# One SBUF ring tile taken earlier, the gate's rounds spaced wider, three transposes of c moved, and one pool shifted, in a fused attention and two-MoE kernel

## The chip, the cores and the metric

The kernel runs on one core of a Trainium2 chip, which has eight. The metric is device microseconds (us) for one execution, start to end; lower is better. Only one core is used, so there is no traffic between cores.

## What is computed

Three stages in a row, all in float32, whose intermediate results never leave the core:

```python
def reference(q, k, v, ...):
    out_up = repeat(sm_attn(mean4(q), mean4(k), mean4(v)), 4)       # pooled attention, 4 tokens to one
    out_local = softmax(where(|i - j| < 4, q k^T / 8, -1e9)) @ v     # attention in a narrow band
    x = (out_up + out_local) as [2304 tokens, 512]
    # soft MoE: 8 experts, 4 slots each
    logits = x @ phi                                # 2304 x 32
    d = softmax(logits, over tokens); slot_input = d.T @ x
    slot_out[e] = relu(slot_input[e] @ w1[e]) @ w2[e]
    x = softmax(logits, over slots) @ slot_out      # c @ slot_out, c is 2304 x 32
    # second MoE: 8 experts, every token through every expert
    P = exp(x @ w_gate - max)
    for _ in range(8):                              # Sinkhorn rounds
        P /= P.sum(1, keepdims=True) + 1e-9
        P /= P.sum(0, keepdims=True) + 1e-9
        P *= N / E
    out = sum over e of P[:, e:e + 1] * (relu(x @ w1[e]) @ w2[e])
```

The second MoE carries nearly all the arithmetic: for each of 8 experts, 2304 x 512 x 1024 and 2304 x 1024 x 512. Its input x has rank 32 (it is c times 32 slot outputs), and the kernel uses that: the first product is (c scaled by the gate) times a small matrix of 32 rows.

## The kernel before

**Stages.** Attention over 16 pairs of heads comes first, then the soft MoE, then the second MoE, which is one long loop over `seq`, 72 steps of (e, p): expert e outside, p one of nine blocks of 256 tokens inside. The instructions of all engines are written out by hand in one order; each engine runs its own in that order and waits for semaphores.

**The first expert (e = 0, steps n = 0 to 8).** Step p runs `y_first(p)`: 48 matmuls of 512 columns that multiply hidden values (tiles `s75` and `s63`, each a high and a low part) with the weights `whi` and `wlo`, in two halves c = 0 and c = 1 of the hidden units. `hidden(0, p, c)` makes the hidden values. The last half, (p, c) = (8, 1), puts them in a tile of their own, `hl` (L957), because `s75` and `s63` are wanted by the second expert by then.

**The gate.** Beside these matmuls runs a generator, `side`: `gate()`, then eight times `sink()`, one Sinkhorn round. It is called once for every two matmuls of `y_first`; each `yield` is one such place. A round puts four short DVE instructions on the gate's tile `pg` (L1132 to L1135), passes 6 places, puts a matmul `sp` with a tile of ones on PE (L1139), passes 2, puts five DVE instructions (L1145 to L1149), passes 5.

**The other experts (e = 1 to 7).** Step (e, p) runs `y_pair(e, p)`: seven products of a Strassen-like scheme, each 12 matmuls of 256 columns, 84 in all, in four PSUM banks: products 7 and 5, then 6 and 3, then 1, then 4 and 2. The stationary operand comes from `s75`, `s63` or `d` (made by `hidden`, `sums`, `direct_hi`, `direct_lo`), the moving one from the weight tile W[e, n] of that product. Hooks at given matmul counts k call the work for the next steps: `hidden` at 2 and 14, `sums` from 19 on, `direct_hi` at 79, and so on.

**The ring of weight tiles.** `w_tile` hands out tiles of 8 KB a partition in turn from a ring of ten: seven buffers of pool `wp`, then three of pool `tp`. Tile number i reuses the buffer of tile i - 10, and its first write waits until the last reader of that one is done. The order decides which tile meets which. Tiles 0 to 7 are the first expert's weights. Each later expert takes seven, in the order 7, 5, 6 (`w_early`, an ACT copy and a POOL subtraction each, in steps p = 5, 6 and 7 of the expert before), 3, 1, 4 (`w_late`, in step p = 8 of the expert before) and 2 (step p = 0 of its own). `hl` is taken when it is written, in step (0, 8): it is tile 11, between 7, 5, 6 (8, 9, 10) and 3, 1, 4, 2 (12 to 15) of expert 1. Expert 2's are 16 to 22.

**c times the gate.** `scale_c(e, p)` multiplies c with the gate's column on POOL into `crp` (two buffers); `turn_c(e, p)` transposes it on PE into the PSUM tile `cq` (pool `xq`, a single buffer), copies it with ACT (L936) and subtracts with DVE (L937) into `ce`, which `hidden(e, p, ...)` reads. For expert 1 these are called in step (0, 8), at k = 2 to 24; `hidden(1, 0, 0)` follows at k = 12.

**Places in SBUF.** The pools lie one behind the other: `wp`, `acc`, `tp`, `rp`, `mm`, `op`. Up to `mm` the sizes are multiples of 512 bytes a partition. `mm` holds `ones` (512), `stack_r` (512), `low_rows` (4, which takes 32), `skew` (32, a tile that no instruction uses), `rs` (72, takes 96), `cs`, `gm`, `g1`, `gn` (32 each), `wf` (4096) and two `crp` (1024 each). So `op`, with the stationary operands, begins 288 bytes past a multiple of 512 from where the weight tiles begin.

Of the kernel before, what the change touches and what calls it, by code (L numbers as in the profile page):

```python
# [8 lines left out]
FP32 = mybir.dt.float32  # L9
# [41 lines left out]
def attn_moe_moe_kernel(  # L51
# [13 lines left out]
    nc = tc.nc  # L65
    B, H, S, D = q.shape
    N, DM = out.shape
    E, _, F = w1a.shape
    NS = phi.shape[1]
    SPE = NS // E  # L70
    HP = H // 2
    NT = N // 128
# [718 lines left out]
    mm = ctx.enter_context(tc.tile_pool(name="mm", bufs=1, reuse_waits="tile"))  # L791
    op = ctx.enter_context(tc.tile_pool(name="op", bufs=3, reuse_waits="tile"))
# [8 lines left out]
    def w_tile(name, dtype=FP32R):  # L801
        nonlocal nt_
        pool = wp if nt_ % NTW < NW else tp
        nt_ += 1
        return pool.tile([128, 2048], dtype, name=name, tag="w")
# [105 lines left out]

    O = {}
    H = {}
    ce = {}
    crp = {}

# [25 lines left out]
    def o_tile(tag, n):  # L942
        return op.tile([128, 2, 2, 128 * n], FP32R, name=tag, tag=tag, bufs=n)

    def hidden(e, p, c):

        ps = hq.tile([128, 2, 512], FP32, name="h", tag="h")
        if e == 0:
            for f in range(4):
                g = 4 * c + f  # L950
                nc.tensor.matmul(  # L951
                    out=ps[:, f // 2, 256 * (f % 2):256 * (f % 2) + 256], lhsT=a4s[:, 0, 128 * g:128 * g + 128],
                    rhs=c4[:, 256 * p:256 * p + 256], start=True, stop=True,
                )
            if (p, c) == (NP - 1, 1):

                t = w_tile("hl")  # L957
                hi, lo = t[:, 0:1024], t[:, 1024:2048]
            else:
                hi, lo = (o_tile(n, 2).rearrange("p a b x -> p (a b x)") for n in ("s75", "s63"))  # L960
            O[0, p, c] = hi, lo
            for j in range(2):
                h = slice(512 * j, 512 * j + 512)
                nc.scalar.activation(out=hi[:, h], in_=ps[:, j], func=ACTF.Relu)  # L964
                relu(lo[:, h], ps[:, j], hi[:, h].bitcast(FP32), ALU.subtract)
            return
        for j in range(2):
            for k in range(2):
                g = 2 * c + j + 4 * k
                nc.tensor.matmul(  # L970
                    out=ps[:, j, 256 * k:256 * k + 256], lhsT=a4s[:, e % 2, 128 * g:128 * g + 128],
                    rhs=ce[e, p], start=True, stop=True,
                )
        r21 = op.tile([128, 2, 128], FP32, name="r21", tag="r21", bufs=2)
        x = op.tile([128, 2, 2, 256], FP32, name="xs", tag="xs", bufs=2)
        H[e, p, c] = ps, x
        A21, A11, A22, A12 = (ps[:, :, 128 * i:128 * i + 128] for i in range(4))
        s3, s1, s2, s4 = (x[:, i // 2, :, 128 * (i % 2):128 * (i % 2) + 128] for i in range(4))
        nc.scalar.activation(out=r21, in_=A21, func=ACTF.Relu)  # L979
        now = c == 0 or (e, p) == (1, 0)  # L980
        if now:
            direct_hi(e, p, c)
        relu(s3, A11, r21, ALU.subtract)
        relu(s1, A22, r21, ALU.add)
        relu(s2, A11, s1, ALU.subtract)
        relu(s4, A12, s2, ALU.add)
        if now:
            direct_lo(e, p, c)

    def sums(e, p, c, i):  # L990

        t = o_tile(("s75", "s63")[i], 2)
        v = H[e, p, c][1][:, i]
        for j, n in enumerate(("75", "63")[i]):
# [4 lines left out]
    def direct_hi(e, p, c):  # L999
        t = H[e, p, c, "d"] = o_tile("d", 3)  # L1000
        for j, n in enumerate("142"):
# [87 lines left out]
            out=out[128 * t:128 * t + 128, :], in_=acc[:, p, h:h + 2, :].rearrange("p q d -> p (q d)")  # L1089
        )  # L1090

    ones = mm.tile([128, 128], FP32, name="ones")
    nc.vector.memset(ones, 1.0)
    stack_r = mm.tile([128, 4, 32], FP32R, name="stack_r")
    nc.vector.tensor_copy(out=stack_r, in_=stack)
    low_rows = mm.tile([128, 1], FP32, name="low_rows")
    mm.tile([128, 8], FP32, name="skew")
    for i in range(4):
        nc.vector.memset(low_rows[32 * i:32 * i + 32], -1.0 if i % 2 else 0.0)

# [30 lines left out]
    def sink():  # L1131
        nc.vector.tensor_reduce(out=rs[:, :, 0], in_=pg, axis=AX.X, op=ALU.add)  # L1132
        nc.vector.tensor_scalar(out=rs, in0=rs, scalar1=EPS, scalar2=None, op0=ALU.add)
        nc.vector.reciprocal(out=rs, in_=rs)
        nc.vector.tensor_tensor(out=pg, in0=pg, in1=rs.to_broadcast([128, NT, E]), op=ALU.mult)  # L1135
        for _ in range(6):
            yield
        sp = xq.tile([128, NT, E], FP32, name="sp", tag="x")
        nc.tensor.matmul(  # L1139
            out=sp.rearrange("p t e -> p (t e)"), lhsT=ones, rhs=pg.rearrange("p t e -> p (t e)"),  # L1140
            start=True, stop=True,
        )
        for _ in range(2):
            yield
        nc.vector.tensor_reduce(out=cs_[:, 0, :], in_=sp.rearrange("p t e -> p e t"), axis=AX.X, op=ALU.add)  # L1145
        nc.vector.tensor_scalar(out=cs_, in0=cs_, scalar1=EPS, scalar2=None, op0=ALU.add)
        nc.vector.reciprocal(out=cs_, in_=cs_)
        nc.vector.tensor_tensor(out=pg, in0=pg, in1=cs_.to_broadcast([128, NT, E]), op=ALU.mult)
        nc.vector.tensor_scalar(out=pg, in0=pg, scalar1=float(N) / E, scalar2=None, op0=ALU.mult)  # L1149
        for _ in range(5):  # L1150
            yield
# [43 lines left out]
    for n, (e, p) in enumerate(seq):  # L1195
        nx, nx3, nx4 = at(n + 1), at(n + 3), at(n + 4)
        hooks = {}

        def hook(k, f, *a):
            hooks.setdefault(k, []).append((f, a))  # L1200

        total = 48 if e == 0 else 84
        fr = (lambda x: x * total // 84)
        if e == 0:
            if n:
                hook(2, hidden, 0, p, 1)
            if n < NP - 1:
                hook(26, hidden, *nx, 0)
            else:
                for k, f, *a in (  # L1210
                    (12, hidden, 0), (14, sums, 0, 0), (22, hidden, 1), (26, sums, 1, 0), (28, sums, 0, 1),
                    (30, sums, 1, 1),
                ):
                    hook(k, f, *nx, *a)
        elif nx:
            for k, f, *a in (
                (2, hidden, 0), (14, hidden, 1), (19, sums, 0, 0), (26, sums, 1, 0), (43, sums, 0, 1),
                (50, sums, 1, 1), (79, direct_hi, 1), (79, direct_lo, 1),
            ):
                hook(k, f, *nx, *a)  # L1220

        if n == NP - 2:

            def first_c():
                make_cx()
                for i in range(2):
                    scale_c(1, i)

            hook(total - 8, first_c)
        if n == NP - 1:  # L1230
            for i in range(2):
                hook(2 + 6 * i, turn_c, 1, i)
                hook(8 + 6 * i, scale_c, 1, 2 + i)
            hook(18, turn_c, 1, 2)
            hook(24, scale_c, 1, 4)
        elif n >= NP:
            if nx3:
                hook(64, turn_c, *nx3)
            if nx4:
                hook(70, scale_c, *nx4)  # L1240
        if nx and nx[0] == 1:
            hook(fr(40), scale_first, nx[1])
        if e + 1 < E:
            if p == 0:
                hook(60, load_w1, e + 1) if e else hook(12, load_w1, e + 1)
            if p in (2, 3):
                hook(fr(10), a_part, e + 1, p - 2)
                hook(fr(34), a_sum, e + 1, p - 2)
            if p == 3:
                hook(fr(30), load_w2, e + 1, 0)  # L1250
                hook(fr(30), load_w2, e + 1, 1)
            if p == 4:
                early = w_early(e + 1)
                hook(fr(60), next, early)
            if p in (5, 6, 7):
                hook(fr(28), next, early)
                hook(fr(56), next, early)
            if p == 8:
                for x, m in (28, "3"), (52, "1"), (72, "4"):
                    hook(fr(x), w_late, e + 1, m)  # L1260
        if e and p == 0:
            hook(8, w_late, e, "2")
        k = 0
        for _ in (y_first(p) if e == 0 else y_pair(e, p)):
            k += 1
            if e == 0 and k % 2 == 0 and (n or k > 6):
                next(side, None)
            if n == 0 and k <= 12:
                if k % 3 == 0:
                    next(soon, None)  # L1270
                if k == 6:
                    hidden(0, 0, 1)
            for f, a in hooks.pop(k, ()):
                f(*a)
        assert not hooks, (e, p, list(hooks))
# [28 lines left out]
```

## Time and profile before

| | us |
|---|---|
| median of three runs | 1084.28 |
| lowest and highest | 1084.22, 1086.52 |
| the profiled execution | 1083.03 |
| its span, first to last instruction | 1081.2 |
| PE busy in the span | 1025.5 (95%) |
| DVE, POOL, ACT busy | 779.0, 649.4, 540.0 |

The profile is one execution. PE is TensorE's matmuls, PEld its weight loads, DVE VectorE, ACT ScalarE, POOL GpSimd. L1064 stands for line 1064 of the kernel. The attention takes the span up to about 190 us, the soft MoE up to about 219, the first expert of the second MoE about 223 to 350, the other seven experts 350 to 1076. The granted clock of TensorE is 1.00 (2.4 GHz) in nearly all of the second MoE.

### The profile page before, as it was taken

What the parts mean: (1) busy time and instruction counts of PE and PEld (TensorE: products, weight loads), DVE (VectorE), ACT (ScalarE), POOL (GpSimd) and SP (SyncE); (2) the same over time, 40 slices, a digit from 0 to 9 for tenths busy, and PEclk for the clock granted to TensorE, in tenths of its full rate; (3) what the DMA queues carried; (4) which work ended last, traced back from release to release, by engine and by line L of the source; (5) the groups of instructions that cost most, each with busy time, mean ns of one, the idle gap of its engine ahead of it and who ended that gap; (6) DMA issues with size and microseconds to landing.
All of it is one profiled execution on the core that took longest, in us unless ns stands there. A gap on an engine that the chain in (4) does not pass through costs nothing.

```text
span 1081.2 us, 22771 instructions
## 1 busy us (share of the span) xinstructions
PE 1025.5 (95%) x9033; PEld 928.0 (86%) x9033; DVE 779.0 (72%) x1521; ACT 540.0 (50%) x1040; POOL 649.4 (60%) x543
## 2 busy tenths in 40 slices
PE   6887988889999999899999999999999999999998
PEld 5675753367787899899999999999999999999998
DVE  4997872155654677677778778778777787788996
ACT  4986750132225556554564456455545564455442
POOL 5655341020044859974897589659946994699452
PEclk8999997889999999999999999999999999999999
DMA  9999998941100220022003100310210022000111
GB/s 190 174 183 234 260 332 320 386 169 40 39 1 1 79 78 2 2 79 79 1 1 118 40 2 8 111 41 1 79 57 24 2 78 79 2 2 21 59 40 60
DMA packets 95919, 93.84 MB, mean 87 GB/s; under 512 B 59076, under 2 KB 64836, under 8 KB 95812
## 3 DMA queue, kind: packets, MB, share of 16 engines
q1 hardware_dynamic: 95812, 92.37, 30.3%
q8 instruction: 72, 1.18, 0.5%
q14 instruction: 35, 0.29, 0.1%
HBM read 87.64 MB, written 4.72 MB: 85 GB/s over the span
## 4 chain that ended last, share of the span: by engine, by line
PE 76%; DVE 3%; POOL 2%; DMA 1%; issue 1%; ACT 1%; ACTq 0%; DVEq 0%; POOLq 0%
PE m L1064 56%; PE y L1021 7%; PE h L970 5%; PE h L712 2%; PE ap L885 1%; DMA w1s<-in_moe_w_dram 1%; PE cq L933 1%; POOL wt L842 1%; POOL s L842 1%; PE h L951 1%; PE so L761 1%; PE as L901 1%; DVE xs L940 1%; DVE acc L1051 0%; DVE d L940 0%
## 5 line engine op out<-in xcount | busy, mean ns | idle before, releaser
L842 POOL TENSOR_TENSOR s<-xs,s 128x512 fp32r<-128x512 f32 x252 | 323.0, 1299 | 192.7 <-ACT s L996 192.7
L1064 PE MATMUL m<-wt,s 128*128 128x256 f32 x3024 | 394.9, 282 | 1.3 <-POOL s L842 1.3
L1064 PEld LDWEIGHTS m<-wt,s 128*128 128x128 f32 x3024 | 374.2, 189 | 12.9 <-issue 10.1
L1064 PE MATMUL m<-wt,d 128*128 128x256 f32 x2268 | 292.3, 283 | 1.2 <-DVE acc L1051 1.2
L1064 PEld LDWEIGHTS m<-wt,d 128*128 128x128 f32 x2268 | 276.6, 188 | 1.6 <-PE m L1064 1.5
L1051 DVE TENSOR_TENSOR acc<-acc,m 128x512 f32<-128x512 f32 x315 | 215.2, 683 | 23.3 <-PE m L1064 10.9
L996 ACT ACTIVATE s<-xs 128x512 fp32r<-128x512 f32 x252 | 155.9, 630 | 104.5 <-DVE xs L940 69.3
L940 DVE SCALAR_TENSOR_TENSOR d<-h,d 128x768 fp32r<-128x768 f32 x126 | 120.0, 953 | 92.8 <-ACT d L1003 92.8
L1003 ACT ACTIVATE d<-h 128x768 fp32r<-128x768 f32 x126 | 102.2, 811 | 74.7 <-PE m L1064 74.7
L940 DVE SCALAR_TENSOR_TENSOR xs<-h,xs 128x256 f32<-128x256 f32 x252 | 107.0, 425 | 8.6
L940 DVE SCALAR_TENSOR_TENSOR xs<-h,r 128x256 f32<-128x256 f32 x252 | 94.7, 418 | 20.8 <-issue 13.3
L1021 PE MATMUL y<-whi,s 128*128 128x512 f32 x272 | 89.4, 407 | 2.1 <-ACT whi L835 2.1
L979 ACT ACTIVATE r<-h 128x256 f32<-128x256 f32 x126 | 48.3, 384 | 83.7 <-PE h L970 83.5
L842 POOL TENSOR_TENSOR wt<-w2r,wt 128x1024 fp32r<-128x1024 f32 x35 | 84.1, 2413 | 7.6 <-ACT wt L848 7.6
L970 PE MATMUL h<-cx,a4s 128*128 128x256 f32 x504 | 81.0, 283 | 2.9 <-DVE d L940 2.9
L970 PEld LDWEIGHTS h<-cx,a4s 128*128 128x128 f32 x504 | 69.4, 190 | 3.3 <-DVE d L940 3.1
L1021 PEld LDWEIGHTS y<-whi,s 128*128 128x128 f32 x272 | 51.0, 192 | 12.5 <-ACT whi L835 2.5
L842 POOL TENSOR_TENSOR wf<-w2r 128x1024 f32<-128x1024 f32 x14 | 33.8, 2414 | 42.9 <-issue 42.9
L964 ACT ACTIVATE s<-h 128x512 fp32r<-128x512 f32 x34 | 20.3, 598 | 73.4 <-PE h L951 56.8
L1021 PE MATMUL y<-wlo,s 128*128 128x512 f32 x136 | 55.4, 408 | 0.0
L936 ACT ACTIVATE cx<-cq 128x256 fp32r<-128x256 f32 x63 | 24.1, 382 | 60.8 <-PE cq L933 60.8
L842 POOL TENSOR_TENSOR wt<-wf,wt 128x1024 fp32r<-128x1024 f32 x14 | 33.7, 2410 | 32.6 <-ACT wt L848 32.6
(206 smaller groups left out, 1152.6 us busy)
## 6 DMA issues: line engine op xcount, KB each, us to landing
wa<-in_moe_w_dram SPq DMA_DIRECT2D x32, 1024.0 KB, 9.4
w1r<-in_moe_w_dram SPq DMA_DIRECT2D x14, 1024.0 KB
w2r<-in_moe_w_dram SPq DMA_DIRECT2D x14, 1024.0 KB, 5.0
vw<-in_v_dram SPq DMA_DIRECT2D x62, 96.0 KB, 6.1
kn<-in_k_dram SPq DMA_DIRECT2D x32, 144.0 KB, 6.0
vg<-in_v_dram SPq DMA_DIRECT2D x16, 288.0 KB
out_dram<-acc SPq DMA_DIRECT2D x18, 256.0 KB, 2.0
qn<-in_q_dram SPq DMA_DIRECT2D x20, 144.0 KB, 7.0
```

The lines of the kernel that those rows point to most:

```text
L712: nc.tensor.matmul(out=h1[32 * j:32 * j + 32, a, :], lhsT=slt[:, j, e, :], rhs=w[:, j % 2, 512 * a:512 * a + 512], start=(e == 0), stop=(e ...
L842: eng.tensor_tensor(out=out, in0=x, in1=y, op=ALU.subtract)
L936: nc.scalar.activation(out=r, in_=cp, func=ACTF.Copy)
L940: nc.vector.scalar_tensor_tensor(out=out, in0=ps_, scalar=0.0, in1=in1, op0=ALU.max, op1=op1)
L964: nc.scalar.activation(out=hi[:, h], in_=ps[:, j], func=ACTF.Relu)
L970: nc.tensor.matmul(out=ps[:, j, 256 * k:256 * k + 256], lhsT=a4s[:, e % 2, 128 * g:128 * g + 128], rhs=ce[e, p], start=True, stop=True,)
L979: nc.scalar.activation(out=r21, in_=A21, func=ACTF.Relu)
L996: nc.scalar.activation(out=t[:, 0], in_=v, func=ACTF.Copy)
L1003: nc.scalar.activation(out=t[:, 0], in_=H[e, p, c][0][:, :, 128:512], func=ACTF.Relu)
L1021: nc.tensor.matmul(out=ys[i], lhsT=l, rhs=r, start=(c == 0 and n == 0), stop=(c == 1 and n == 11))
L1051: nc.vector.tensor_tensor(out=v, in0=v, in1=ps, op=op_)
L1064: nc.tensor.matmul(out=ps[:, place], lhsT=l, rhs=W[e, n][:, r, j, :], start=(m == 0), stop=(m == 11))
```

## The change

Four edits. First, `hl`'s tile is taken from the ring at the start of step n = 3, ahead of expert 1's tiles; it becomes tile 8, and expert 1's 7, 5, 6 become 9, 10, 11. All numbers from 12 on are as before. No instruction moves for that. Second, `ones` moves from `mm` to the first buffer of `r21` in `op`, and `skew` grows from 32 to 480 bytes, so `op` begins 64 bytes lower. Third, a Sinkhorn round passes 9 places instead of 6 ahead of its matmul. Fourth, in step (0, 8) the calls of `turn_c` for blocks 0, 1, 2 go from k = 2, 8, 18 to 6, 11, 20 and those of `scale_c` for blocks 2, 3, 4 from 8, 14, 24 to 8, 13, 22.

```diff
+    hl = []
@@ hidden
             if (p, c) == (NP - 1, 1):
-                t = w_tile("hl")
+                t = hl[0]
                 hi, lo = t[:, 0:1024], t[:, 1024:2048]
@@
-    ones = mm.tile([128, 128], FP32, name="ones")
+    ones = op.tile([128, 128], FP32, name="ones", tag="r21", bufs=2)
     nc.vector.memset(ones, 1.0)
@@
-    mm.tile([128, 8], FP32, name="skew")
+    mm.tile([128, 120], FP32, name="skew")
@@ sink
-        for _ in range(6):
+        for _ in range(9):
             yield
         sp = xq.tile([128, NT, E], FP32, name="sp", tag="x")
@@ the loop over seq
         if n == NP - 1:
-            for i in range(2):
-                hook(2 + 6 * i, turn_c, 1, i)
-                hook(8 + 6 * i, scale_c, 1, 2 + i)
-            hook(18, turn_c, 1, 2)
-            hook(24, scale_c, 1, 4)
+            for k, i in (6, 0), (11, 1), (20, 2):
+                hook(k, turn_c, 1, i)
+                hook(k + 2, scale_c, 1, 2 + i)
@@
+        if n == 3:
+            hl.append(w_tile("hl"))
```

## Rows read from the trace of the kernel before

**Rows 1.** Page: engines' busy us; costly group: busy, mean ns, idle before.

```profile
PE 1025.5 (95%) x9033; PEld 928.0 (86%) x9033; DVE 779.0 (72%) x1521; ACT 540.0 (50%) x1040; POOL 649.4 (60%) x543
...
L1064 PE MATMUL m<-wt,s 128*128 128x256 f32 x3024 | 394.9, 282 | 1.3 <-POOL s L842 1.3
```

**Rows 2.** Waits of PE, 226 to 1077 us: total, times, longest.

```profile
PE h L970 <- DVE d L940: 2.9, 1, 2.9
PE y L1021 <- ACT whi L835: 2.1, 1, 2.1
PE cq L933 <- DVE cx L937: 1.4, 1, 1.4
PE m L1064 <- POOL s L842: 1.3, 1, 1.3
PE m L1064 <- DVE acc L1051: 1.2, 2, 0.6
PE sp L1139 <- DVE pg L1135: 1.1, 2, 0.8
```

**Rows 3.** Chain of work, 440 to 470 us: start, us, what.

```profile
442.25 0.22 PE cq L933 x2
...
449.90 1.22 PE h L970 x4
...
457.90 0.22 PE cq L933 x2
...
469.01 0.22 PE cq L933 x2
```

**Rows 4.** Timeline (start, us, instruction, [idle before]); windows (five engines' busy, clock, DMA).

```profile
446.83 1.06 ACT L848 ACTIVATE wt<-wf 128x1024 fp32r<-128x1024 f32 x1 [4.90 <-PE m L1064]
...
442.00:458.00 16.00, 13.06 (x100) 12.86 (x99) 9.06 (x17) 7.81 (x12) 14.31 (x12) 0.89 0.00 1
```

**Rows 5.** Timeline at the two late Sinkhorn matmuls.

```profile
256.43 0.48 PE L1139 MATMUL sp<-pg,ones 128*128 128x144 f32 x2 [0.27 <-DVE pg L1135]
...
278.36 2.41 POOL L842 TENSOR_TENSOR wf<-w2r 128x1024 f32<-128x1024 f32 x1 [42.94 <-issue]
278.94 1.86 DVE L1133 TENSOR_SCALAR rs<-rs 128x18 f32<-128x18 f32 x1
...
281.59 0.48 PE L1139 MATMUL sp<-pg,ones 128*128 128x144 f32 x2 [0.83 <-DVE pg L1135]
```

**Rows 6.** Timeline of step (0, 8): the second transpose of c.

```profile
338.66 0.43 DVE L937 TENSOR_TENSOR cx<-cq,cx 64x256 fp32r<-64x256 f32 x1
...
339.23 0.41 PE L933 MATMUL cq<-ident,crp 128*128 128x128 f32 x2 [1.43 <-DVE cx L937]
...
340.40 0.64 PE L970 MATMUL h<-cx,a4s 128*128 128x256 f32 x4
```

**Rows 7.** Timeline of POOL in step (0, 8).

```profile
343.75 1.30 POOL L842 TENSOR_TENSOR s<-xs,s 128x512 fp32r<-128x512 f32 x1 [6.58 <-ACT s L996]
345.01 0.62 POOL L922 TENSOR_TENSOR crp<-lnat,pg 128x256 f32<-128x256 f32 x1
```

**Rows 8.** Matmul rates: chain 1050 to 1082, then `y` and `as`.

```profile
1058.21 18.24 PE m L1064 x154
...
325.72 0.40 PE L1021 MATMUL y<-wlo,s 128*128 128x512 f32 x1
...
328.52 0.40 PE L1021 MATMUL y<-wlo,s 128*128 128x512 f32 x1
...
346.20 0.39 PE L1021 MATMUL y<-wlo,hl 128*128 128x512 f32 x1
...
348.92 0.39 PE L1021 MATMUL y<-wlo,hl 128*128 128x512 f32 x1
...
262.55 0.47 PE as L901 x2
...
488.87 0.47 PE as L901 x2
```

## The prediction

> **What bounds the kernel now.** I read the page first. PE is busy 95% of the span [rows 1], and from about 350 us on its largest group, the `m` matmuls of L1064, runs almost without idle time: 1.3 us of waiting over 3024 matmuls. So two things can move the time: the few places where PE stands still, and the rate at which its matmuls follow each other. Next I read PE's waits over the second MoE [rows 2]. The reader sees a short list: 10.0 us in six kinds, with 2.9 us in one single wait of an `h` matmul for DVE at the top. Three of the six kinds are touched by the change: that one, `cq <- DVE cx` with 1.4, and `sp <- DVE pg` with 1.1. `m <- POOL s` and `m <- DVE acc` lie behind POOL in the turn from the first expert to the second, and are touched in passing. The wait for `whi` lies at the start of the first expert and is not touched.
>
> **The ring tile (edit 1).** In the chain, `cq` of one step comes at 442.25, of the next at 457.90, of the one after at 469.01 [rows 3]: one step takes 15.65 us, its neighbour 11.11, so 15.65 - 11.11 = 4.54 us are lost in it. The cause stands in ACT's row [rows 4]: the split of a weight tile (L848) begins at 446.83, after 4.90 us of waiting for an `m` matmul of PE. By the code this is `w_early`'s third split for expert 2, product 6, called at k = 56 of step (1, 7). It is tile 18, and tile 18 - 10 = 8 is product 7 of expert 1, last read at k = 12 of step (1, 8). ACT works in order, so its `cx` copy and `direct_hi` for the next half queue up behind the split, DVE's `direct_lo` behind those, and PE's second `hidden` at k = 14 behind DVE: that is the 2.9 us [rows 2]. While PE stands, its clock falls: the window 442 to 458 has a mean granted clock of 0.89 [rows 4], so part of it ran at 1.2 GHz, and the first `h` group after the wait takes 1.22 us. The other 4.54 - 2.9 = 1.6 us are that.
>
> With `hl` as tile 8, tile 18 meets `hl`, whose last reader is the last matmul of step (0, 8), some 90 us earlier. The split then starts when ACT comes to it. What is late next? The later tiles meet product 7 (tile 19, split at k = 28, freed at k = 12), 5 (split at 52, freed at 24), 6 (72, 36) and 3 (8 of the next step, 48), the pattern that all later experts have, and they show no such wait (the `h` wait occurs once) [rows 2]. `hl` itself takes over a buffer of `tp` without an earlier `w_tile` in it; expert 1's 5 and 6 move onto the two `w1s`, last read before the first `y`. I take the whole: **-4.5 us**. If a new wait took its place, it would be at most the same again.
>
> **The gate's places (edit 3).** PE waited 1.1 us in two of the eight rounds, 0.27 and 0.83 [rows 5]. Three places more are six `y` matmuls, at 2.80 us for 12 [rows 8] 1.40 us, more than either wait. The four DVE instructions and the DVE work queued among them get that much longer; PE runs `y` meanwhile. The gate ends eight times 1.40 = 11 us later, at about 314 us; its first reader on POOL (`crp` for expert 1, called at k = 40 of step (0, 7)) comes some 20 us behind. The second wait was made by one slow instruction: a TENSOR_SCALAR of 18 numbers took 1.86 us beside a POOL subtraction of 2.41 us [rows 5]. The rounds that move later run into more of these splits, so I let one such wait of up to 0.8 us come back in the bound. **-1.1 us**, between -1.4 (the clean gaps) and -0.3.
>
> The Trainium skill ("SBUF — State Buffer", section "Who interferes with whom") says that DVE and GpSimd share a pair of ports, exclusively for a whole instruction, so the second to start waits for the first. The long row is in accord with that; by it a round that meets a POOL split pays up to the split's length, and three places would not cover every meeting. That changes this term by less than 1 us.
>
> **The turns of c (edit 4).** `cq` has one buffer. The second transpose waited 1.43 us for DVE's subtraction of the first, which sat behind `hl`'s two evictions and began at 338.66 [rows 6]. This chain starts from `hidden(0, 8, 1)` and does not move: it ends at 338.66 + 0.43 = 339.09. What changes is how much PE does before it must wait: with 6 and 11 instead of 2 and 8, three more matmuls of 0.233 us (0.70 us) come ahead of the wait, and `hidden(1, 0, 0)` at k = 12 stands one matmul behind the second transpose instead of four. It was issued at 340.40 [rows 6]; now about 339.7. So PE still waits, but 0.7 us less. POOL gains more. It was idle 6.58 us before the first `s` subtraction at 343.75 and then ran `crp` for 0.62 us at 345.01 [rows 7]; that `crp` (block 3, from k = 14, behind `sums`, to 13, ahead of it) now falls into the idle time. POOL's following work, on which PE waits with `m <- POOL s` (1.3 us) and, through DVE, `m <- DVE acc` [rows 2], comes 0.7 + 0.6 = 1.3 us earlier. PE cannot gain more than that there: **-1.2 us**, between -0.6 (only the first wait) and -2.0 (all of the two waits that follow, less what PE itself comes earlier). If POOL's idle time were not there, the `crp` would cost its 0.6 us again.
>
> **The shift of 64 bytes (edit 2).** From the sizes in the code, `op` began 288 bytes past the weight tiles, modulo 512; with `ones` out (512) and `skew` 448 larger it is 224, or the weights 288 past `op`. No instruction is added. The only question is whether PE's rate depends on where its two operands lie. `m` runs at 18.24 / 154 = 118.4 ns; `y` from `s75` and `s63` (288 apart) at 2.80 / 12 = 233 ns, `y` from `hl` (same pool as its weights, 0 apart) at 2.72 / 12 = 227 ns [rows 8]. So it may, by 6 ns in 233, or 2.8%. The nearest row to the new distance is `as`: for the first experts its operands are `stack_r` and `aps`, 224 apart, and two matmuls take 0.47 us; from the third expert on they are 0 apart and also take 0.47 [rows 8]. So distance 224 costs nothing there against 0, within 5 ns. I take **0**. The ends: the seven experts have 63 x 84 = 5292 `m` matmuls, 627 us at 118.4 ns, and 2.8% of them is 17.5 us either way.
>
> The Trainium skill ("TensorE: Matmul & The Clock Gate", section "Step-by-step: what each phase is for") says that weight loads and the moving operand have separate SBUF read ports and so do not slow each other; by that rule the shift is worth nothing, as I take it. The two rates of `y` speak against it being the whole story, so I keep the ends.
>
> **The sum.** -4.5 - 1.1 - 1.2 + 0 = -6.8 us. The profiled execution took 1083.03, 1.8 around its span, and becomes 1076.2; it lay 1.25 below the median, so on the median 1084.28 the forecast is 1077.5 us.
>
> **Rivals.** (a) The shift speeds PE up: `op`'s new distance is as good for `m` as 0 is for `y`. For it: the 227 ns. Against: `as`. By 1 ns in 118 it is worth 5.3 us, in full 17.5: 1060 to 1075, most likely about 1070. (b) The shift slows PE down: weight loads and moving stream collide more. Place: every `m` matmul. It decides against the kernel from 6.8 us / 5292 = 1.3 ns a matmul on; at half the bound, 1.6 ns, +8.7 us, 1086.2; in full 1095. For it: PE's rate is the bound for 700 us, so nothing hides it. Against: the `as` row. (c) The ring only passes the wait on: another split in steps (1, 7) and (1, 8) meets a busy tile. Then the -4.5 are lost and 1082.0 remains. Against: the freed and split counts above. (d) `skew`, which no instruction uses, takes no room; then the distance stays and the forecast stands, since its term is 0.
>
> **How the numbers follow.** Forecast with (d): 0.54; (a) 0.25; (b) 0.13; (c) 0.08. The range takes the gain of (a) down to 1066 (beyond lies about 0.07) and (b) up to 1083 (beyond lies 0.1): 1066 to 1083. What a measurement can tell from no change is about 0.2%, 2.2 us: faster is below 1082.1, slower above 1086.4. Faster: the forecast, (a), half of (c) and a little of (b): 0.85. Same: half of (c) and the part of (b) between 1082 and 1086: 0.09. Slower: the rest of (b): 0.06.
>
> **What the new profile would show.** Edit 1: no ACT wait at L848 near 440 us, steps of 11.1 us throughout from (1, 4) on, clock 1.00. Edit 3: no `sp <- DVE pg`. Edit 4: `cq <- DVE cx` near 1 us instead of 1.4, `crp` ahead of the first `s` on POOL, `m <- POOL s` under 0.8. Edit 2: 154 `m` matmuls at the end in 18.24 us; 17.5 would mean rival (a), 18.6 rival (b). The forecast is wrong if that last number moves.

## The result, and the profile after

The kernel after takes 1070.26 us (median of four runs, 1066.78 to 1071.43) against 1085.40 for the kernel before: a ratio of 0.985, with a 95% interval of 0.982 to 0.988. It is 15.1 us faster where 6.8 were forecast: the time lies inside the range of the prediction, but the gain is 2.2 times the one forecast. The profiled execution took 1071.43 us, with a span of 1069.7.

First the page of the kernel after (busy us of the engines; then the costliest matmul group, as in [rows 1]). A line is 1 to 2 higher in number than before from `hidden` on.

```profile
PE 1018.8 (95%) x9033; PEld 920.0 (86%) x9033; DVE 780.5 (73%) x1521; ACT 539.1 (50%) x1040; POOL 649.4 (61%) x543
...
L1065 PE MATMUL m<-wt,s 128*128 128x256 f32 x3024 | 389.1, 280 | 1.0 <-POOL s L842 1.0
```

PE is busy 6.7 us less with the same 9033 instructions, and the 3024 `m` matmuls of this group 5.8 us less. That speaks for more than waits that went away: the matmuls themselves follow each other faster. The waits of PE in the second MoE, in total, times and the longest, answer to [rows 2] (the one for `whi`, at the start of the first expert, left out):

```profile
PE m L1065 <- DVE acc L1052: 1.1, 2, 0.7
PE cq L934 <- DVE cx L938: 1.0, 1, 1.0
PE m L1065 <- POOL s L842: 1.0, 1, 1.0
PE m L1065 <- POOL wt L842: 0.5, 1, 0.5
```

The 2.9 us of `h` and the 1.1 us of `sp` are gone; `cq` fell from 1.4 to 1.0, and `m <- POOL s` from 1.3 to 1.0 (the prediction wanted it under 0.8); one wait is new, of `m` for `wt` on POOL. The chain of work, in one ordinary step and at the end, answers to [rows 3] and [rows 8]:

```profile
545.50 0.22 PE cq L934 x2
...
550.64 5.84 PE m L1065 x50
556.48 0.22 PE cq L934 x2
...
1046.94 17.98 PE m L1065 x154
```

A step is 556.48 - 545.50 = 10.98 us, before 11.11; the last 154 `m` matmuls run at 116.8 ns, before 118.4.

To see where the 15 us come from I take the start of the first matmul of each step from the records of both profiled executions; a step's length is the difference of two.

| stretch | before | after | change |
|---|---|---|---|
| up to the first `y` (attention, soft MoE) | 226.02 | 229.30 | +3.28 |
| (0, 0) | 16.51 | 16.09 | -0.42 |
| (0, 1) to (0, 7), the gate's | 92.29 | 90.82 | -1.47 |
| (0, 8) and (1, 0), the turns of c | 27.91 | 26.61 | -1.30 |
| (1, 8) and (2, 0), the ring | 26.77 | 23.50 | -3.27 |
| an ordinary step, for example (5, 5) | 11.11 | 10.98 | -0.13 |
| (2, 1) to the last `m` | 604.72 | 597.08 | -7.64 |

The first two rows are no part of the change: over the executions profiled for this study the first `y` starts between 220.2 and 229.6 us, and step (0, 0) takes 16.0 to 17.0. The steps (1, 1) to (1, 7), which the table leaves out, take 0.72 us less. From the first `y` to the last `m` it is 850.14 against 835.33, 14.8 us less, and 8 of them (63 steps of 0.13) are the pace of `m`. In the last row 0.92 us belong to the single step (7, 1), 11.90 us before and 10.98 after, of which more below.

### The profile page after: what moved, and what is told of

Read it like the earlier page. It is cut to its first block, busy times and chain, and to the rows that moved or that the text cites. A ratio compares the mean times of both kernels' runs of the same rounds, so it can differ in the third digit from the quotient of the medians.

```text
span 1069.7 us, 22765 instructions
## 1 busy us (share of the span) xinstructions
PE 1018.8 (95%) x9033; PEld 920.0 (86%) x9033; DVE 780.5 (73%) x1521; ACT 539.1 (50%) x1040; POOL 649.4 (61%) x543
## 4 chain that ended last, share of the span: by engine, by line
PE 79%; POOL 7%; DMA 5%; DVE 3%; ACT 2%; SPq 2%; issue 1%; POOLq 0%; ACTq 0%; DVEq 0%
PE m L1065 52%; PE y L1022 9%; PE h L971 5%; POOL s L842 3%; POOL wt L842 2%; DMA kn<-in_k_dram 2%; PE ap L885 1%; PE h L712 1%; DMA w1s<-in_moe_w_dram 1%; PE cq L934 1%; DMA wa<-in_moe_w_dram 1%; PE loc L465 1%; PE h L952 1%; PE so L761 1%; SPq L222 1%
## 5 line engine op out<-in xcount | busy, mean ns | idle before, releaser
L1065 PE MATMUL m<-wt,s 128*128 128x256 f32 x3024 | 389.1, 280 | 1.0 <-POOL s L842 1.0
L1065 PEld LDWEIGHTS m<-wt,s 128*128 128x128 f32 x3024 | 369.5, 188 | 12.5 <-issue 10.1
L1065 PE MATMUL m<-wt,d 128*128 128x256 f32 x2268 | 289.4, 282 | 1.6 <-DVE acc L1052 1.1
L1065 PEld LDWEIGHTS m<-wt,d 128*128 128x128 f32 x2268 | 273.8, 188 | 2.2 <-PE m L1065 1.5
```

The lines of the kernel that those rows point to most:

```text
L1065: nc.tensor.matmul(out=ps[:, place], lhsT=l, rhs=W[e, n][:, r, j, :], start=(m == 0), stop=(m == 11))
```

## The experiments

### The ring alone

```diff
 # before, plus
+        if n == 3:
+            hl.append(w_tile("hl"))
```

> The kernel before with edit 1 alone (hl takes its ring tile at n = 3). Theory: the 4.54 us of step (1, 8) go, but POOL, which had used that stall to catch up, is behind in steps (1, 8) and (2, 0), as the kernel after shows it there (0.69 + 0.85 us over its own pace), so 3 us net, and 118.4 ns for an m matmul stays. Rival A, my forecast: the whole 4.5 us. Rival B: the ring carries more than half of the 15 us; then over 7 us, and m would have to run faster.

Measured: 1080.48 us against 1085.69, ratio 0.995 (0.992 to 0.998). Steps (1, 8) and (2, 0) take 11.35 and 11.85 us instead of 15.67 and 11.10, ordinary ones 11.11 as before: 3.6 us are won there, 1.0 us stays over two ordinary steps. That lies between the 3 us of the theory and the 4.5 of rival A. The wait of PE that is new:

```profile
PE m L1065 <- POOL wt L842: 0.4, 1, 0.4
```

So the wait for the tile goes, as forecast, and a smaller one for POOL comes: 4.5 us were too many. Rival B falls: the ring does not carry half of the gain.

### The shift alone, and half of it

```diff
 # shift_only: before, with both lines; ones_only: with the first
-    ones = mm.tile([128, 128], FP32, name="ones")
+    ones = op.tile([128, 128], FP32, name="ones", tag="r21", bufs=2)
-    mm.tile([128, 8], FP32, name="skew")
+    mm.tile([128, 120], FP32, name="skew")
```

> The kernel before with edit 2 alone (ones into r21's buffer, skew 480 bytes): stationary operands 224 bytes past the weight tiles, modulo 512, instead of 288. Theory: m runs at 116.7 ns instead of 118.4, a step of 84 at 10.98 us instead of 11.11, 8 us in all; the stall of step (1, 8) stays. Rival: the rate comes from elsewhere (fewer stalls, other edits); then 118.4 ns and no gain.

> The kernel before with half of edit 2: ones in r21's buffer, skew as before. The order of the tiles in op changes (r21 comes first), the distance stays 288. Theory (the distance counts): 118.4 ns, no change of time. Rival (which buffers lie where counts): 116.7 ns and 8 us faster, as with the whole of edit 2.

Measured: shift_only 1074.97 us against 1085.69, ratio 0.989 (0.984 to 0.994); ones_only 1081.12, ratio 0.997 (0.994 to 1.001), not told from no change. An ordinary step takes 10.98 us with the shift and 11.11 with `ones` moved alone; the stall of (1, 8) stays in both (15.74 and 15.85). An ordinary step of shift_only in the chain:

```profile
563.29 0.22 PE cq L933 x2
...
574.27 0.22 PE cq L933 x2
```

The whole gain in pace comes with 64 bytes, and not with the new order of the tiles in `op`. The last 154 `m` matmuls, by which the prediction wanted to be judged, take 18.17 us in shift_only and not 17.98, because step (7, 7) takes 10.95 us there instead of 10.76; the ordinary steps are the safer sign.

### Everything 64 bytes higher

```diff
 # after, with
-    const.tile([128, 8], FP32, name="line")
+    const.tile([128, 24], FP32, name="line")
```

> The kernel after with the unused tile line 64 bytes larger, at the very front: weights and stationary operands all lie 64 bytes higher, the distance of 224 stays, and the stationary operands are back at their old remainder of 416 modulo 512. Theory (distance): as the kernel after, 116.7 ns. Rival (the stationary operand's own place modulo 512 counts): 118.4 ns, about 9 us slower than the kernel after.

Measured: 1070.11 us, ratio to the kernel before 0.984 (0.980 to 0.988); an ordinary step takes 10.98 us. Weights and stationary operands lie where they did not before, 224 apart, and the pace is that of the kernel after. For this distance and this one move the distance counts, not the place.

One rival is left: the shift moves `op` against the tiles of the other engines too, so the collision could be with their accesses and not between the two operands of PE. The second half of `y` in step (0, 8) speaks against it: there both operands lie among the weight tiles, 0 apart in every kernel, and the starts of its matmuls are 227 to 228 ns apart on average at all ten distances tried below, while `y` from `op` changes with the distance.

### Other distances

```diff
 # after, with skew of 64, 80, 88, 96, 104, 112, 128, 32 words
-    mm.tile([128, 120], FP32, name="skew")
+    mm.tile([128, 64], FP32, name="skew")
```

> The kernel after with skew of 256 bytes: stationary operands 0 bytes past the weight tiles modulo 512. Question: how the pace of m goes with the distance. If the row of y from hl (227 ns against 233) were a guide for m, 0 would be the best distance: about 115 ns, a step of 10.8 us. If y and m are limited by different things, as the unchanged 233 ns of y in the kernel after suggests, m at 0 can be anything from 114 to 120 ns; the h matmuls, also of 256 columns and at distance 0, run at 119 to 120.

> The kernel after with skew of 384 bytes: distance 128 modulo 512. If only the distance modulo 128 counts, the same pace of m as at 0, 256 and 384, to 0.2 ns. Otherwise another.

> The kernel after with skew of 512 bytes: distance 256 modulo 512. If only the distance modulo 128 counts, the pace of m at 0 and 128; if it changes smoothly with the distance, between those at 224 (116.7 ns) and 288 (118.4), 117.5 ns.

> The kernel after with skew of 128 bytes: distance 384 modulo 512. If only the distance modulo 128 counts, the pace of m at 0; if it changes smoothly from 288 on, more than 118.4 ns, and PE slower than in the kernel before.

> The kernel after with skew of 320 bytes: distance 64 modulo 512. If the pace depends on the distance from a multiple of 128 alone, the same as at 192; if it goes up steadily from 32 (118.4 ns) to 128 (120.1), about 119.

> The kernel after with skew of 448 bytes: distance 192 modulo 512. The distances tried so far repeat modulo 256: 0 and 256 give 120.1 ns for m, 128 and 384 also 120.1, 32 (that of the kernel before) 118.4, 224 116.7. If distances below a multiple of 256 are good and 224 is no single spot, 192 lies between 116.7 and 120.1; if 224 is a narrow dip, 120.

> The kernel after with skew of 352 bytes: distance 96 modulo 512. If the pace goes by the distance from a multiple of 128 alone, 96 is as 224: steps of 10.98 us. If it repeats only modulo 256, anything between 11.0 (64) and 11.21 (128).

> The kernel after with skew of 416 bytes: distance 160 modulo 512. If the pace goes by the distance from a multiple of 128 alone, 160 is as 32 and 288: steps of 11.11 us. If it falls from 128 (11.21) by 192 (11.06) to 224 (10.98), about 11.14.

Measured, one execution each: the distance of the stationary operand past the weight tile, modulo 512, the ordinary step (5, 5), and 50 `m` matmuls in a row as the chain has them (us). The distance in the kernel before is 288, shown as 32.

| distance | step | 50 `m` |
|---|---|---|
| 0 | 11.25 | 6.00 |
| 256 | 11.25 | 6.00 |
| 32 (288, the kernel before) | 11.11 | 5.91 |
| 64 | 11.01 | 5.89 |
| 96 | 11.14 | 5.94 |
| 128 | 11.21 | 6.01 |
| 384 | 11.21 | 6.01 |
| 160 | 11.21 | 6.00 |
| 192 | 11.06 | 5.89 |
| 224 (the kernel after) | 10.98 | 5.84 |

In both pairs tried, distances that are equal modulo 256 agree: 0 and 256, 128 and 384. It is no smooth curve: there are two dips, around 64 and around 224, with 0 and 128 to 160 the worst. Over all 63 steps the spread is (11.25 - 10.98) x 63 = 17 us, and 224 has the shortest step (5, 5) of the ten. The guess by a multiple of 128 alone holds roughly and not exactly (32 and 160 differ by 0.10 us a step, 96 and 224 by 0.16).

The distance does not fix the pace alone. At 64 the ordinary steps alternate between 11.00 and 11.06 us. At 192 the pace changed within one execution, while the granted clock stayed at 1.00. Up to step (7, 1) the `m` matmuls start 117.7 ns apart (mean over those in a row); in it PE waits 3.0 us for DVE; in the steps behind it they mostly start 114.3 ns apart, the fastest of all runs, and the step is down to 10.89 us. The last 154 of dist_192, where the kernel after has 17.98:

```profile
1051.67 17.65 PE m L1065 x154
```

What sets the one pace or the other was not tested. If 114.3 ns could be held over all 5292 `m` matmuls, it would be worth another 13 us by this estimate, so it is open whether 224 is the best place.

The `y` matmuls of 512 columns rank the distances in another way. Their rows in the chain, first at distance 0 (dist_0):

```profile
316.66 5.47 PE y L1022 x24
```

and at 224 (the kernel after):

```profile
319.10 5.60 PE y L1022 x24
```

For `y`, 0 is better (228 ns against 233); for `m` it is the worst. At 192 both are near their best: `y` takes 229 ns.

### The gate and the turns alone

```diff
 # before, with edits 3 and 4
-        for _ in range(6):
+        for _ in range(9):
...
+            for k, i in (6, 0), (11, 1), (20, 2):
+                hook(k, turn_c, 1, i)
+                hook(k + 2, scale_c, 1, 2 + i)
```

> The kernel before with edits 3 and 4 alone. Theory: the two waits of sp go (steps p = 2 and 3 of the first expert together 1.4 to 1.8 us shorter, as in the kernel after), steps (0, 8) and (1, 0) together 1.2 to 1.3 us shorter; the stall of step (1, 8) of 4.5 us and 118.4 ns for m stay. Rival: part of the gain at (0, 8) and (1, 0) in the kernel after came from edit 1 or 2; then less than 0.8 us there.

Measured, one execution of 1074.94 us: (0, 2) and (0, 3) take 14.25 and 14.01 us instead of 14.79 and 15.32, 1.85 less, (0, 6) 0.23 more; (0, 8) and (1, 0) 26.67 instead of 27.91, 1.24 less; ordinary steps 11.11. Both edits do in this kernel what they do in the kernel after. One thing more is to be seen at (1, 8), where the old stall stays. The waits of PE, and the window around it (busy time of five engines, granted clock, DMA share, GB/s):

```profile
PE h L970 <- DVE d L940: 2.9, 1, 2.9
...
436.00:452.00 16.00, 13.06 (x110) 12.83 (x110) 8.95 (x17) 9.09 (x15) 14.31 (x11) 1.00 0.00 1
```

The same wait of 2.9 us, but here the granted clock stays at 1.00, and the step loses 14.39 - 11.11 = 3.3 us, not 4.56. So 1.3 us of the stall in the kernel before (the prediction had 1.6) were the clock at 1.2 GHz after it, and whether the clock falls differs between executions: in shift_only and ones_only it fell after the same wait.

### What was left of the stall

```diff
 # acc_on_dve: after, with; acc_mixed: nc.vector for p < 5, nc.gpsimd above
-            sub(nc.gpsimd, acc[:, p, q], acc[:, p, V], acc[:, p, q])
+            sub(nc.vector, acc[:, p, q], acc[:, p, V], acc[:, p, q])
```

> The kernel after, with the two subtractions of scale_first (128x256 each, once in each step of expert 1) on DVE instead of POOL. Theory: the 1.5 us that steps (1, 8) and (2, 0) still lose in the kernel after are POOL's backlog of expert 1, in which it is busy without a break from 435 to 471 us; 1.45 us less of POOL work a step takes it away: both at 10.98 us, 1.5 us faster. Rival: DVE pays more than POOL gives, since two operands in SBUF make it wait for POOL (0.43 us alone, 1.24 us and more beside POOL in the last expert), and PE then waits for DVE; then steps of expert 1 over 10.98 and no gain.

> The kernel after, with scale_first's subtractions on DVE for the blocks p = 0 to 4 and on POOL for 5 to 8. On DVE for all blocks, steps (1, 0) and (1, 1) became 0.4 and 0.7 us shorter, (1, 5) to (1, 7) 1.3 to 1.8 us longer, where the pair took 3.24 us on DVE beside POOL's splits. Theory: this keeps the first and drops the second, about 1.1 us faster than the kernel after, and part of the backlog in (1, 8) and (2, 0) stays, since the late subtractions are on POOL. Rival: without the late ones nothing is won at (1, 0) and (1, 1) either; then as the kernel after.

> The kernel after, unchanged, for a comparison on the same chip: steps of 10.98 us, (1, 8) and (2, 0) at 11.7 and 11.8.

Measured: acc_on_dve 1070.89 us, ratio to before 0.989 (0.985 to 0.993). Step (2, 0) is 10.98 us and (1, 8) 11.29, in accord with a backlog of POOL as the cause. The test is not clean: (1, 5) to (1, 7) take 12.3 to 12.7, and this longer time alone lets POOL catch up. DVE there, and POOL at the same time:

```profile
418.95 3.24 DVE L842 TENSOR_TENSOR acc<-acc 128x256 f32<-128x256 f32 x2 [0.73 <-ACT acc L1038]
...
418.08 2.40 POOL L842 TENSOR_TENSOR wt<-wf,wt 128x1024 fp32r<-128x1024 f32 x1
```

The same two instructions take 0.75 us on DVE when POOL is idle as they start. The rival's price is there, and larger than the gain. acc_mixed wins the 0.4 and 0.7 us at (1, 0) and (1, 1) and keeps 10.98 us at (1, 5) to (1, 7), as expected; (1, 8) and (2, 0) stay at 11.68 and 11.83 us, so what is moved of the first five blocks does not reach the backlog. In time it is 1069.75 us against 1069.92 for the kernel after on the same chip, no difference that the runs can tell.

### A step of 17 us that comes and goes

In the profiled execution of acc_mixed, and in that of shift_only, step (7, 1) takes 16.98 us instead of 10.98. DVE and POOL of acc_mixed there:

```profile
970.29 5.69 DVE L842 TENSOR_TENSOR acc<-acc 128x256 f32<-128x256 f32 x1
...
970.12 5.00 POOL L842 TENSOR_TENSOR s<-xs,s 128x512 fp32r<-128x512 f32 x4
```

A subtraction of the last expert's result, with both inputs in SBUF, that takes 0.43 us alone, takes 5.69 while POOL runs four of its own in a row. In the kernel after it met the same four and took 1.37; there it was POOL's four that took longer, 5.49 us. In 19 profiled executions the subtraction was on DVE; it took 5.6 to 5.7 us in three (acc_mixed, shift_only, dist_192) and 1.1 to 1.4 in the others. The step's 6.0 us come in two parts. PE first waits, for a DVE instruction that is queued behind the subtraction:

```profile
PE h L971 <- DVE d L941: 3.1, 1, 3.1
```

The gap between two of its `m` matmuls grows by 3.8 us in all; the 22 behind it run at 1.2 GHz, 213 ns each, and cost another 2.1 (mean granted clock of the step 0.80). In dist_192 the clock stayed at 1.00 after a wait of 3.0 us.

```diff
 # last_on_pool: acc_mixed, with, for R and for Q
-                    sub(nc.vector, av[:, R], av[:, V], av[:, R])
+                    sub(nc.gpsimd if p < 8 else nc.vector, av[:, R], av[:, V], av[:, R])
```

> acc_mixed, and the subtractions of the last expert (128x256, two in each step (7, p)) for p = 0 to 7 on POOL instead of DVE. Theory: the 5.69 us that one of them took on DVE at 970.3 in acc_mixed is a wait for POOL, which ran four subtractions in a row just then; on POOL the step (7, 1) is 10.98 us in every execution, and times of about 1069 us or less come with no 6 us outliers. Rival: POOL's own queue then delays its s subtractions, PE waits for POOL in steps (7, 1) to (7, 8), and nothing is gained.

> The kernel after, unchanged, on the same chip as last_on_pool: about 1070 us, 1 us above last_on_pool in the median if the theory there holds.

Measured: 1070.26 us (1067.54 to 1071.65) against 1068.39 (1064.55 to 1071.40) for the kernel after on the same chip. All steps from (7, 0) to (7, 5) take 10.98 us and PE waits for none of this, so the subtraction is off the path. But (7, 1) is 10.98 us in all three profiled executions of the kernel after, so one execution of this kernel does not show that the long step cannot come. From the first `y` to the last `m` it is 834.96 us against 835.75: a gain of 0.8 us, under what the runs can tell. No version beat the kernel after by a measured amount.

## Why the prediction was wrong

**The shift (edit 2): the failed step.** The prediction put the term at 0 us, because the `as` row at distance 224 took no longer than the one at 0; it brought 8. `as` was nearest in distance and not in form: it has 512 columns, as `y` has. Two `as` matmuls take 0.47 us with either kernel, while `m` went from 118.4 to 116.8 ns. Nor was the row fine enough: 5 ns in 235 is 2%, and the change of `m` is 1.4%. And at 0 apart `as` takes 235 ns where `y` takes 227, so it did not show the one effect that the trace had.

The trace did hold a row of `m`'s shape at a second distance, which the prediction did not use: `h`, 256 columns with its operands 0 apart, at 0.48 us for four, 120 ns each, against 118.4 for `m` at 288. It says that 256 columns depend on the distance too, and the other way round than `y`. It says nothing of 224. So the term had a range and no likeliest value of 0, and the chance of 0.25 for (a) was too low for something that nothing in the trace could settle.

Rival (a) had the right sign by a wrong argument, that `m` at 224 would be as good as `y` is at 0; for `m`, 0 is the worst distance. That its likeliest time, about 1070, is the time measured is luck. The bound of 17.5 us either way was wide: from the distance of the kernel before, the steps in the table above reach 8 us down and 9 us up.

Why 256 columns behave otherwise than 512 is not shown. By the records the weight load for the next matmul starts 2 to 3 ns (median) behind the start of a matmul and lasts 188 ns; that is longer than the 117 ns to the next `m` and shorter than the 233 to the next `y`. So a delayed load might hold up `m` and be hidden in `y`, but which access meets which was not measured.

The Trainium skill ("TensorE: Matmul & The Clock Gate", section "Step-by-step: what each phase is for") has two independent read ports, so that loading the next weights doesn't slow the running matmul. Here one and the same instruction stream changes its pace from 116.8 to 120 ns with the distance between the places of the two operands; the measurement decides, and in this kernel the two reads are not independent.

**The ring (edit 1): mechanism right, size off.** The split found its tile free and started on time: in the kernel after ACT's row at (1, 7) has no wait, where [rows 4] had 4.90 us.

```profile
441.46 1.05 ACT L848 ACTIVATE wt<-wf 128x1024 fp32r<-128x1024 f32 x1
...
452.62 0.71 PE L1065 MATMUL m<-wt,d 128*128 128x256 f32 x4 [0.45 <-DVE acc L1052]
...
444.00:456.00 12.00, 11.55 (x99) 11.37 (x99) 8.62 (x16) 8.04 (x13) 12.00 (x10) 1.00 0.01 1
```

The term was -4.5 and came to -3.0 (26.77 - 23.50 less 0.26 for the pace). A third of the term did not come. The step that failed in it is the question "what is late next", which was answered from the ring's slots and from the later experts. But expert 1 has work that they do not have: `scale_first`'s two subtractions on POOL in each step, 1.45 us. POOL is busy all 12 us of the window above, and in the kernel before it had used PE's stall to catch up. ring_only shows 1.0 us of this at a step of 11.11 us; the kernel after 1.5, since PE comes faster; dist_0, at 11.25 a step, only 0.35. That the loss shrinks as PE comes later is what a backlog would do. That `scale_first` makes the backlog is argued from its 1.45 us a step: in acc_on_dve, which takes it from POOL, the loss at (2, 0) is gone, but PE is late there as well.

**The gate (edit 3): right, a little small.** Forecast -1.1, found -1.5 in the stretch. Both waits of `sp` are gone. The wait column counts 0.27 and 0.83 us; measured by the distance of the starts, (0, 2) and (0, 3) won 1.8, and 0.25 came back at (0, 6), where a later round now is.

**The turns of c (edit 4): right.** Forecast -1.2, found -1.3 (0.13 of it the pace of `m`): -0.71 in (0, 8), where 0.7 were forecast for the first wait, and -0.59 in (1, 0). PE in the kernel after, then POOL, as in [rows 6] and [rows 7]:

```profile
340.64 0.41 PE L934 MATMUL cq<-ident,crp 128*128 128x128 f32 x2 [1.02 <-DVE cx L938]
...
341.12 0.64 PE L971 MATMUL h<-cx,a4s 128*128 128x256 f32 x4
...
341.19 0.62 POOL L923 TENSOR_TENSOR crp<-lnat,pg 128x256 f32<-128x256 f32 x1 [1.97 <-PE cq L934]
344.47 1.30 POOL L842 TENSOR_TENSOR s<-xs,s 128x512 fp32r<-128x512 f32 x1 [2.66 <-ACT s L997]
```

The transpose still waits for the same DVE subtraction, 0.4 us less; `hidden` follows it after one matmul; and `crp` sits in POOL's idle time ahead of the first `s`.

The three terms for waits thus came to -5.8 against -6.8 forecast, and the term that was set to 0 to -8. The 0.8 us that are left of the 14.8 are within what steps (0, 0) and (7, 1) differ by between executions.

## What to carry to other kernels

When PE is the bound and its matmuls are short, put the distance of the stationary and the moving operand on the list of things to measure: the size of an unused tile moved the time by 1.1% here (shift_only), and the step by up to 2.5% (10.98 to 11.25 us); no row of another shape tells the sign. When a stall goes, ask which engine used it to catch up, and look at the work of that very stretch, not at stretches that look alike. And a two-input DVE instruction is cheap only where GpSimd is idle: look at what runs beside it before counting it.

## What the runs showed of the hardware

The pace of back-to-back 128x256 fp32r matmuls changes with the distance of their operands, the same for the two pairs that are equal modulo 256 bytes: 116.8 ns at 224, 120 at 0, 256, 128 and 384. At 192 it was 117.7 ns and, behind a stall in the same execution, mostly 114.3. With 512 columns it is 228 ns at 0, 229 at 192 and 233 at 32 and 224.

A DVE instruction with two inputs in SBUF can wait for more than the GpSimd instruction beside it: 5.69 us beside four GpSimd instructions of 1.25 us each. The Trainium skill ("SBUF — State Buffer", section "Who interferes with whom") has a two-input DVE instruction contend with a GpSimd instruction that reads SBUF, for a pair of ports that one of them locks; the row agrees in kind, and shows the wait to last over a chain of them.

A wait of PE of 2.9 to 3.1 us occurred seven times in the steps (1, 8) and (7, 1) of the profiled executions. Behind five the granted clock fell to 1.2 GHz (a mean of 0.80 to 0.89 over the step: before, ones_only, acc_mixed, and both in shift_only); behind two it stayed at 1.00 (gate_turn, dist_192).
